# At most two of the first 24 loads in flight, in a fused decay-attention and FFN kernel

## The chip, the cores and the metric

The kernel runs on one core of one Trainium2 chip. The metric is the device time of one execution in microseconds; for the kernel before it is the median of three runs. Profiles come from one profiled execution each.

## The reference, cut to what matters

Attention with a decay per head, over blocks with a carried state, is followed by a feed-forward network with a squared relu. All is float32.

```python
# q, k, v: (4, 8, 768, 64); lam: (8,); w_in: (512, 2048); w_out: (2048, 512)
for b in range(nb):                                   # blocks of 64 positions
    intra = einsum('bhic,bhjc->bhij', qb, kb) * Dmask      # Dmask: lam ** (i - j) for i >= j
    intra = einsum('bhij,bhjd->bhid', intra, vb)
    inter = einsum('bhid,bhde->bhie', qb * lam_pow, kv_state)
    out[:, :, sl] = intra + inter
    kv_state = lam_block * kv_state + einsum('bhsd,bhse->bhde', kb * rev_pow, vb)
x = out, as (3072, 512)                               # 4 x 768 tokens, 8 heads of 64
h = maximum(x @ w_in, 0)
return h * h @ w_out
```

## The kernel before, in words

**Tiles.** The 3072 tokens are cut into 24 chunks of 128, and three chunks make one tile of 384 tokens, eight tiles in all. For a chunk, attention runs in four parts on TensorE, all on matmuls of 64x64 (L302): an opening of 64 matmuls as the profile counts them (scores and new states, `open`), and a result in two halves (`result(0, ..)` with the states' part, `result(1, ..)`). Between the opening and the result VectorE masks the scores (s, L363) and adds up the states (hold, L355, L361); ScalarE copies the first state of a sequence (hold, L354). Between the two halves of the result stands a one-element copy on ScalarE, the dot (L401). Then VectorE multiplies the result by the decay (xr, two steps, L409), and xr is split into a high and a low part (xs: ScalarE's cast L415, VectorE's subtraction L416) which are the FFN's input. Before the opening, the chunk's values are scaled by powers of lam: for the first six chunks by six steps on ScalarE (L329) and one on VectorE (L331).

**FFN.** For each tile and each of 16 slices f of the hidden size, TensorE multiplies the inputs by the slice's first weight (L433: wih high, wil low), ScalarE applies relu and square (g, gh: L447 to L452), VectorE makes the low part (gl, L454), and TensorE multiplies by the second weight (L439, L440, L442: woh, wol).

**Weights.** Each weight slice is loaded once (st, L278), 512 KB, and split into its high and low part in place: an absolute value on ScalarE (L279), four steps on VectorE (L280 to L286), a cast on ScalarE (L288) and a subtraction on VectorE (L290). There are three st and three m buffers. Tile 0 and tile 1 use the weights while they arrive.

**Loads.** All loads leave from SyncE's queue, 512 KB each: st for a weight, ka and qv for a chunk (L316, L317). The first 24 by the order of issue before: 1, 2 the two weights of slice 0; 3 to 6 ka and qv of chunks 0 and 1; 7 slice 1's first weight; 8 to 11 chunks 2 and 3; 12 slice 1's second weight; 13 to 16 chunks 4 and 5; 17, 18 slice 2's weights; 19 to 22 chunks 6 and 7; 23, 24 slice 3's weights. Besides them ScalarE loads the small table lamx, from which GpSimd makes the powers (L236, L250).

**What sets the order.** Every step is first recorded with an engine, a duration, a key (when it is due) and its buffers, and a planner (`Plan.order`) lays all of them out by list scheduling with these durations and with a latency per engine (LAT). Each engine's instructions are then written out in that order, and each engine runs its own strictly in that order, waiting on semaphores where data or buffers are needed. The planner also puts filler matmuls on zeros (L240, L243) where it sees TensorE idle before its time 140. `in_turn` keeps the loads of chunks in sequence. The semaphores of loads are eight counters in rotation (DMAHW0 to DMAHW7, the first taken by lamx), so a load also waits until the eighth load before it has landed.

Of the kernel before, what the change touches and what calls it, by code (L numbers as in the profile page):

```python
# [55 lines left out]
class Plan:  # L56


    LAT = {"PE": 0.22, "ACT": 0.14, "DVE": 0.13, "POOL": 0.12, "SP": 2.0}

    def __init__(self):
        self.ops, self.slots = [], {}
# [4 lines left out]
    def op(self, eng, dur, key, fn, deps=(), bufs=(), after=(), lat=None, mode=None):  # L67
        o = Op(eng, dur, key, fn, [d for d in deps if d is not None], list(bufs), [d for d in after if d is not None], lat or self.LAT[eng], mode)
        for b in o.bufs:
            b.left += 1  # L70
        self.ops.append(o)
        return o

    def order(self, pe_slow, fill, begin):
        need, out = {}, {}
        for o in self.ops:
            both = set(map(id, o.deps)) | set(map(id, o.after))
            need[id(o)] = len(both)
            for d in both:
                out.setdefault(d, []).append(o)  # L80
        ready = {e: [o for o in self.ops if o.eng == e and not need[id(o)]] for e in self.LAT}
        free = dict(dict.fromkeys(self.LAT, 0.0), **begin)
        slots = {k: [(0.0, i) for i in range(n)] for k, n in self.slots.items()}
# [68 lines left out]
FIRST, SLOW_STEP, LAG, BEGIN2, CHUNK, STEP = 18.0, 6.5, 16, 9.0, 3.0, 4.8  # L152
PE_SLOW, FILL_END, FILL, FILL_REST, SWITCH = 6.5, 140.0, 0.215, 0.1, 0.18
XOFF = 16
VS = 6
AFTER = NF - 2


def tt(n):

    return 0.066 + n / 960


def act(n):

    return 0.085 + n / 1200
# [6 lines left out]
def kernel(ctx: ExitStack, tc: tile.TileContext, ka, qv, lamx, w, out):  # L173
    nc = tc.nc
    const = ctx.enter_context(tc.tile_pool(name="const", bufs=1))
    ps = ctx.enter_context(tc.tile_pool(name="ps", bufs=1, space=PSUM))
    plan = Plan()
# [25 lines left out]
    mask = const.tile([P, HC], F32, name="mask")  # L203
    xs = const.tile([P, XOFF + 2 * SLOTS["x"] * NCC * N], F32R, name="xs")
    tiles["x"] = [[xs[:, XOFF + (2 * i + t) * NCC * N:XOFF + (2 * i + t + 1) * NCC * N].rearrange("p (c i) -> p c i", c=NCC) for t in range(2)] for i in range(SLOTS["x"])]
    dot = const.tile([P, 1], F32, name="dot")
# [12 lines left out]
    def at(b):  # L219
        return tiles[b.kind][b.slot]  # L220
# [14 lines left out]
    def power(hs):  # L235
        nc.gpsimd.tensor_tensor(out=wdec[:, hs], in0=lam[:, hs], in1=ej[:, hs], op=ALU.pow)  # L236
# [7 lines left out]

    plan.filler = filler

    o_start = plan.op("POOL", 4.95, -99, start_tables)
    o_pow = plan.op("POOL", 1.6, -98, lambda: power(slice(0, H)), [o_start])
    o_pow2 = plan.op("POOL", 1.6, -97, lambda: power(slice(H, 2 * H)), [o_pow])
    o_lc = plan.op("POOL", 1.01, -96, lambda: nc.gpsimd.tensor_tensor(out=lc, in0=lam[:, 2 * H:2 * H + NP], in1=ec, op=ALU.pow), [o_pow2])  # L250
# [2 lines left out]
    def turned():  # L253
# [3 lines left out]
    o = plan.op("DVE", 0.4, -5, lambda: nc.vector.tensor_copy(  # L257
        at(wb).rearrange("p (s d) -> p s d", d=D), wdec[:, H:2 * H].unsqueeze(2).broadcast_to([P, H, D])), [o_pow2], [wb])
    o_turned = o = plan.op("PE", 0.9, 3, turned, [o], [wb, rps], mode="F")
    o_rdec = plan.op("DVE", tt(512), 3, lambda: nc.vector.tensor_tensor(  # L260
        out=rdec, in0=at(rps).rearrange("p (n i) -> p n i", n=NCC), in1=lam[:, 2 * H + NP:].unsqueeze(2).broadcast_to([P, NCC, C]), op=ALU.mult), [o], [rps])

    def weights(f, i, key, load_key):
        def part(k):
            return (wih[f].rearrange("p c f -> p (c f)"), wil[f].rearrange("p c f -> p (c f)"), woh[f], wol[f])[2 * i + k]

        st, m = Buf("st"), Buf("m")

        def words(t):
            return at(st).bitcast(U32).rearrange("p (n t) -> p n t", t=2)[:, :, t]  # L270

        def bits():
            return at(m).bitcast(U32)

        def add(eng, dur, fn, deps, bufs, lat=None):
            return plan.op(eng, dur, key, fn, deps, bufs, lat=lat)

        o = plan.op("SP", 1.28, load_key, lambda: nc.sync.dma_start(out=at(st), in_=w[f, i]), [], [st])  # L278
        o = add("ACT", 0.56, lambda: nc.scalar.activation(at(m), words(1).bitcast(F32), AF.Abs), [o], [st, m])  # L279
        o = add("DVE", 0.336, lambda: nc.vector.tensor_scalar(  # L280
            out=at(m), in0=at(m), scalar1=W_MIN, scalar2=W_MAX, op0=ALU.max, op1=ALU.min), [o], [m])
        o = add("DVE", 0.336, lambda: nc.vector.tensor_scalar(  # L282
            out=bits(), in0=bits(), scalar1=3, scalar2=0x3FFFFFF8, op0=ALU.logical_shift_left, op1=ALU.bitwise_and), [o], [m])
        o = add("DVE", tt(512), lambda: nc.vector.scalar_tensor_tensor(  # L284
            out=bits(), in0=words(1), scalar=0xC0000000, in1=bits(), op0=ALU.bitwise_and, op1=ALU.bitwise_or), [o], [st, m])
        o = add("DVE", tt(512), lambda: nc.vector.scalar_tensor_tensor(  # L286
            out=bits(), in0=words(0), scalar=29, in1=bits(), op0=ALU.logical_shift_right, op1=ALU.bitwise_or), [o], [st, m])
        oh = add("ACT", act(512), lambda: nc.scalar.copy(part(0), at(m)), [o], [m])  # L288
        oh.late = f >= F_LATE
        ol = add("DVE", tt(512), lambda: nc.vector.tensor_tensor(out=part(1), in0=at(m), in1=part(0), op=ALU.subtract), [oh], [m])  # L290
        return oh, ol
# [3 lines left out]
    def in_turn(name, o):  # L295
        if turn.get(name):
            o.after.append(turn[name])
        turn[name] = o
        return o
# [4 lines left out]
    class Chunk:  # L304
# [8 lines left out]
            self.blocks = 2 if self.c < NC_ - 1 else 1  # L313

        def load(self, key):
            self.o_ka = in_turn("load", plan.op("SP", 1.28, key, lambda: nc.sync.dma_start(out=at(self.ka), in_=ka[self.i]), [], [self.ka]))  # L316
            self.o_qv = in_turn("load", plan.op("SP", 1.28, key, lambda: nc.sync.dma_start(out=at(self.qv), in_=qv[self.i]), [], [self.qv]))  # L317

        def vals(self):
            return at(self.qv)[:, 1].rearrange("p n (h d) -> p n h d", h=2)  # L320
# [4 lines left out]
        def weighted(self, key):  # L325
            v = lambda: at(self.qv)[:, 1].rearrange("p n (h d) -> p (n h) d", h=2)
            split = VS if self.i < N_ALONE else 0

# [154 lines left out]
    for f in range(NF):  # L483
        t = FIRST + f * SLOW_STEP
        ws.append((weights(f, 0, t - 7, -30 + ws_at[f]), weights(f, 1, t - 2, -30 + ws_at[f] + (3.5 if f == 1 else 0.5))))
# [3 lines left out]
    for i in range(len(CHUNKS)):  # L489
        ti, j = i // NT, i % NT  # L490
        if i < N_ALONE:
            key = i * CHUNK if ti == 0 else BEGIN2 + (i - NT) * CHUNK
        else:
            k = ti - 1 if j else max(ti - 2, 1)
            key = begin[k] + per[k] * ((0.5, 4.5, 8.5) if k == 1 and ti == 2 else (12.5, 3.5, 8.0))[j]
# [4 lines left out]
    for i, ch in enumerate(chunks):  # L500
# [4 lines left out]
        key = nxt.key if nxt else ch.key + 0.2 if i < N_ALONE else begin[ti - 1] + 12.5 * per[ti - 1]  # L505
# [55 lines left out]
```

## Time and profile before

| | before |
|---|---|
| median of 3 runs | 619.06 us (617.88 to 619.86) |
| the profiled execution | 618.99 us, its span 617.3 us |
| TensorE matmul busy | 606.9 us, 98% of the span |
| VectorE, ScalarE busy | 298.0 us (48%), 215.1 us (35%) |
| loads and stores | 49.06 MB |
| mean granted TensorE clock | 0.992 |

Busy time of TensorE is modelled and says little about where it is slow; the views by stretch of time and the chain of waits say more. In the rows quoted below a view of groups or of time gives the line in the program, the engine (PE is TensorE, PEld its weight loads, DVE VectorE, ACT ScalarE, SPq SyncE's queue), the operation, output<-input by name, and xcount.

### The profile page before, as it was taken

The page shows a single profiled execution, that of the slowest core. Times are in us where ns is not written, and L with a number is a line of the kernel's source. Part 1 is how long each engine was busy: PE and PEld are TensorE (multiplying, and loading weights), DVE is VectorE, ACT ScalarE, POOL GpSimd, SP SyncE. Part 2 cuts the span into 40 slices and gives each one's busy share as a digit, 9 for nine tenths or more (in the row PEclk, how much of TensorE's full clock was granted, in tenths as well). Part 3 has the DMA queues.
Part 4 walks back from the last instruction along what each step waited for, and adds up shares of the span by engine and source line. Part 5 has one row for each costly group of instructions (what it writes and reads, how often), then busy time and mean ns, then how long its engine had stood idle before and what let it go on. Part 6 is the DMA issues. An engine that isn't in the chain of part 4 may idle for free.

```text
span 617.3 us, 12907 instructions
## 1 busy us (share of the span) xinstructions
PE 606.9 (98%) x5686; PEld 538.4 (87%) x5686; DVE 298.0 (48%) x612; ACT 215.1 (35%) x450; POOL 5.7 (1%) x10
## 2 busy tenths in 40 slices
PE   8799999999999999999999999999999999999997
PEld 4489998888898898988899998989888989899996
DVE  6689999965233444343343442434443423232223
ACT  5547767743341222221223232222223222232221
POOL 3000000000000000000000000000000000000000
PEclk9789999999999999999999999999999999999999
DMA  8914555424020121110121120111110000010001
GB/s 342 401 48 165 175 172 179 163 103 150 30 81 29 58 69 70 51 71 20 50 70 51 70 69 1 69 52 69 71 61 36 26 1 1 2 51 1 0 2 51
DMA packets 15175, 49.06 MB, mean 79 GB/s; under 512 B 1808, under 2 KB 1808, under 8 KB 15120
## 3 DMA queue, kind: packets, MB, share of 16 engines
q1 hardware_dynamic: 14976, 48.24, 21.4%
q8 instruction: 44, 0.72, 0.5%
q14 instruction: 11, 0.09, 0.0%
q10 hardware_dynamic: 144, 0.01, 0.0%
HBM read 41.96 MB, written 6.29 MB: 78 GB/s over the span
## 4 chain that ended last, share of the span: by engine, by line
PE 96%; DMA 2%; DVE 1%; issue 1%; ACT 0%; ACTq 0%
PE bank L433 44%; PE bank L439 15%; PE bank L442 14%; PE bank L440 14%; PE bank L302 8%; DMA ka<-ka 1%; DMA g<-lamx 1%; PE bank L243 1%; DVE m L284 0%; DVE xr L472 0%; DVE s L363 0%; DVE xr L409 0%; DVE rdec L260 0%; DVE m L282 0%; DVE hold L361 0%
## 5 line engine op out<-in xcount | busy, mean ns | idle before, releaser
L433 PE MATMUL bank<-xs,wih 128*128 128x384 f32 x1024 | 200.7, 338 | 0.0
L433 PEld LDWEIGHTS bank<-xs,wih 128*128 128x128 f32 x1024 | 180.6, 188 | 6.0
L453 DVE TENSOR_TENSOR g<-g 128x384 f32<-128x384 f32 x96 | 53.5, 557 | 212.7 <-ACT gh L452 167.2
L447 ACT ACTIVATE g<-bank 128x384 f32<-128x384 f32 x128 | 62.8, 490 | 267.0 <-PE bank L433 267.0
L439 PE MATMUL bank<-woh,gh 128*128 128x512 f32 x384 | 152.3, 397 | 0.0
L440 PE MATMUL bank<-wol,gh 128*128 128x512 f32 x384 | 150.8, 393 | 0.0
L433 PE MATMUL bank<-xs,wil 128*128 128x384 f32 x512 | 110.0, 337 | 0.0
L442 PE MATMUL bank<-woh,gl 128*128 128x512 f32 x384 | 109.4, 393 | 0.0
L433 PEld LDWEIGHTS bank<-xs,wil 128*128 128x128 f32 x512 | 91.0, 188 | 0.0
L442 PEld LDWEIGHTS bank<-woh,gl 128*128 128x128 f32 x384 | 71.9, 188 | 16.4 <-DVE gl L454 0.5
L439 PEld LDWEIGHTS bank<-woh,gh 128*128 128x128 f32 x384 | 72.0, 188 | 15.0 <-ACT gh L450 0.6
L440 PEld LDWEIGHTS bank<-wol,gh 128*128 128x128 f32 x384 | 72.1, 188 | 13.6
L454 DVE TENSOR_TENSOR gl<-g,gh 128x384 fp32r<-128x384 f32 x128 | 71.2, 556 | 16.0 <-ACT gh L450 10.0
L452 ACT ACTIVATE gh<-g 128x384 fp32r<-128x384 f32 x96 | 50.3, 524 | 3.0
L355 DVE TENSOR_TENSOR hold<-bank,hold 128x256 f32<-128x256 f32 x40 | 16.8, 420 | 34.5 <-PE bank L302 34.5
L302 PE MATMUL bank<-qv,ka 64*64 64x64 f32 x1472 | 29.0, 228 | 2.4 <-issue 2.4
L415 ACT CAST xs<-xr 128x512 fp32r<-128x512 f32 x24 | 14.9, 621 | 44.2 <-DVE xr L409 44.1
L302 PEld LDWEIGHTS bank<-qv,ka 64*64 64x64 f32 x1472 | 26.8, 144 | 3.7 <-issue 3.7
L302 PEld LDWEIGHTS bank<-s,qv 64*64 64x64 f32 x768 | 17.2, 139 | 11.7 <-issue 8.7
L302 PE MATMUL bank<-s,qv 64*64 64x64 f32 x768 | 23.1, 232 | 2.7 <-issue 1.8
L331 DVE TENSOR_TENSOR qv<-qv,wdec 128x512 f32<-128x512 f32 (+1 forms) x24 | 14.1, 590 | 24.0 <-DMA qv<-qv 23.9
L279 ACT ACTIVATE m<-st 128x512 f32<-128x512 f32 x32 | 21.5, 674 | 9.4 <-DMA st<-w 8.0
(46 smaller groups left out, 300.7 us busy)
## 6 DMA issues: line engine op xcount, KB each, us to landing
st<-w SPq DMA_DIRECT2D x32, 512.0 KB, 3.4
ka<-ka SPq DMA_DIRECT2D x24, 512.0 KB, 3.9
qv<-qv SPq DMA_DIRECT2D x24, 512.0 KB, 5.2
out<-ob SPq DMA_DIRECT2D x23, 256.0 KB, 2.1
out<-xr SPq DMA_DIRECT2D x1, 256.0 KB, 2.0
g<-lamx ACTq DMA_DIRECT2D x1, 12.0 KB, 4.3
```

The source lines that it names most:

```text
L279: o = add("ACT", 0.56, lambda: nc.scalar.activation(at(m), words(1).bitcast(F32), AF.Abs), [o], [st, m])
L302: nc.tensor.matmul(*args, **kw, skip_group_check=True)
L355: return plan.op("DVE", tt(256), key, lambda: nc.vector.tensor_tensor(out=at(new), in0=u(t), in1=at(old), op=ALU.add), [o] + deps, [self.s ...
L415: oh = plan.op("ACT", act(512), key2, lambda: nc.scalar.copy(at(x)[0][:, :, cs], at(xr)), os_, [xr, x])
L433: nc.tensor.matmul(at(h)[:, 0:N], wt[:, cc, :], xt[:, cc, :], start=k == 0, stop=k == 3 * NCC - 1)
L439: nc.tensor.matmul(at(os_[j]), at(gh)[:, sl], woh[f], start=f == 0, stop=False)
L440: nc.tensor.matmul(at(os_[j]), at(gh)[:, sl], wol[f], start=False, stop=False)
L442: nc.tensor.matmul(at(os_[j]), at(gl)[:, sl], woh[f], start=False, stop=f == NF - 1)
L447: orr = plan.op("ACT", 0.49, key, lambda: nc.scalar.activation(at(g), at(h)[:, 0:N], AF.Relu), [o1], [h, g, run])
L452: ogh = plan.op("ACT", 0.525, key, lambda: nc.scalar.activation(at(gh), at(g), AF.Square), [orr], [g, gh])
L453: og = plan.op("DVE", 0.555, key, lambda: nc.vector.tensor_tensor(out=at(g), in0=at(g), in1=at(g), op=ALU.mult), [orr, ogh], [g])
L454: ogl = plan.op("DVE", 0.555, key, lambda: nc.vector.tensor_tensor(out=at(gl), in0=at(g), in1=at(gh), op=ALU.subtract), [og, ogh], [g, gh, ...
```

## The change

Three things are altered. Each load is passed through a new function `loaded`: load 3 to load 24, by the order in which they are written out, gets a wait on the landing of the load two before it. The planner's cost of a load on SyncE rises from 1.28 to 1.65 and SyncE's latency from 2.0 to 2.3; GpSimd's first step is costed at 5.2 in place of 4.95. So the planner writes another order on all engines. The work on data is the same.

```diff
-    LAT = {"PE": 0.22, "ACT": 0.14, "DVE": 0.13, "POOL": 0.12, "SP": 2.0}
+    LAT = {"PE": 0.22, "ACT": 0.14, "DVE": 0.13, "POOL": 0.12, "SP": 2.3}
...
+PACE, PACED, LOAD = 2, 24, 1.65
...
-    o_start = plan.op("POOL", 4.95, -99, start_tables)
+    o_start = plan.op("POOL", 5.2, -99, start_tables)
...
+    loads = []
+
+    def loaded(d):
+
+        loads.append(d.ins)
+        if PACE < len(loads) <= PACED:
+            tc.add_manual_dep(d.ins, loads[-1 - PACE].name, mybir.DependencyInfo(mybir.DependencyClass.Sync, mybir.DependencyReason.DATA), reason="pace")
...
-        o = plan.op("SP", 1.28, load_key, lambda: nc.sync.dma_start(out=at(st), in_=w[f, i]), [], [st])
+        o = plan.op("SP", LOAD, load_key, lambda: loaded(nc.sync.dma_start(out=at(st), in_=w[f, i])), [], [st])
...
-            self.o_ka = in_turn("load", plan.op("SP", 1.28, key, lambda: nc.sync.dma_start(out=at(self.ka), in_=ka[self.i]), [], [self.ka]))
+            self.o_ka = in_turn("load", plan.op("SP", LOAD, key, lambda: loaded(nc.sync.dma_start(out=at(self.ka), in_=ka[self.i])), [], [self.ka]))
```

The load of qv is altered as that of ka is. Lines of the program move down by one up to the new function and by nine behind it.

SyncE's queue at its start, before; the names in brackets are the landing counters and engines that a load waits for:

```order
L278 DMA st_134<-w 128x512
L316 DMA ka_0_148<-ka 128x1024
L317 DMA qv_0_154<-qv 128x1024
L316 DMA ka_1_149<-ka 128x1024
L317 DMA qv_1_155<-qv 128x1024
L278 DMA st_135<-w 128x512
L316 DMA ka_2_150<-ka 128x1024 [waits DMAHW0_49]
L317 DMA qv_2_156<-qv 128x1024 [waits DMAHW1_49]
```

And now:

```order
L287 DMA st_134<-w 128x512
L325 DMA ka_0_148<-ka 128x1024 [waits DMAHW1_49]
L326 DMA qv_0_154<-qv 128x1024 [waits DMAHW2_49]
L325 DMA ka_1_149<-ka 128x1024 [waits DMAHW3_49]
L326 DMA qv_1_155<-qv 128x1024 [waits DMAHW4_49]
L287 DMA st_135<-w 128x512 [waits DMAHW5_49]
L325 DMA ka_2_150<-ka 128x1024 [waits DMAHW6_49,DMAHW0_49]
L326 DMA qv_2_156<-qv 128x1024 [waits DMAHW7_49]
```

The order of these loads is kept; each now waits for the landing two before it, where before the eighth load before it was waited for. Further down, load 19 is now slice 3's first weight and the loads of chunks 6 and 7 are 20 to 23.

TensorE at the first FFN product (xs with wih_69 and wil_70), before; qv_4 is chunk 4's buffer, qv_3 with s_2 and s_3 the second half of chunk 3's result:

```order
L302 MATMUL bank_63<-qv_4_158,ka_4_152 64x64 x2
L302 MATMUL bank_61<-qv_4_158,ka_4_152 64x64 x2
L302 MATMUL bank_62<-s_2_122,qv_3_157 64x64 x2
L302 MATMUL bank_68<-s_3_123,qv_3_157 64x64 x2
L302 MATMUL bank_62<-s_2_122,qv_3_157 64x64 x2
L302 MATMUL bank_68<-s_3_123,qv_3_157 64x64 x2
L433 MATMUL bank_65<-xs,wih_69 128x384 x8
L433 MATMUL bank_65<-xs,wil_70 128x384 x4
```

And now:

```order
L244 MATMUL bank_63<-ob_114 64x128 x2
L442 MATMUL bank_63<-xs,wih_69 128x384 x8
L442 MATMUL bank_63<-xs,wil_70 128x384 x4
L311 MATMUL bank_62<-s_2_122,qv_3_157 64x64 x2
L311 MATMUL bank_68<-s_3_123,qv_3_157 64x64 x2
L311 MATMUL bank_62<-s_2_122,qv_3_157 64x64 x2
L311 MATMUL bank_68<-s_3_123,qv_3_157 64x64 x2
L311 MATMUL bank_61<-qv_4_158,ka_4_152 64x64 x2
L311 MATMUL bank_64<-qv_4_158,ka_4_152 64x64 x2
```

The product now stands ahead of the second half of chunk 3's result and of chunk 4's opening, which both stood before it. Ahead of it there are 30 rows of fillers in place of 23.

ScalarE at the relu of the third FFN product and the absolute value of load 24 (m_138<-st_134; g_111<-bank_68 before and g_111<-bank_66 now are relus), before:

```order
L288 CAST wih_77<-m_138 128x512
L447 ACTIVATE g_111<-bank_68 128x384
L288 CAST woh_79<-m_136 128x512
L449 ACTIVATE g_111<-g_111 128x384
L279 ACTIVATE m_138<-st_134 128x512
L450 CAST gh_107<-g_111 128x384
```

And now:

```order
L297 CAST wih_77<-m_138 128x512
L424 CAST xs<-xr_1_161 128x4x128
L288 ACTIVATE m_138<-st_134 128x512
L456 ACTIVATE g_111<-bank_66 128x384
L297 CAST woh_79<-m_136 128x512
L458 ACTIVATE g_111<-g_111 128x384
L459 CAST gh_107<-g_111 128x384
```

The absolute value that needs load 24 moved ahead of a relu, its square and the cast that follow.

More of the change, by code (lines that the diff above doesn't have):

```diff
@@ L315, in load @@
         def load(self, key):
-            self.o_ka = in_turn("load", plan.op("SP", 1.28, key, lambda: nc.sync.dma_start(out=at(self.ka), in_=ka[self.i]), [], [self.ka]))
-            self.o_qv = in_turn("load", plan.op("SP", 1.28, key, lambda: nc.sync.dma_start(out=at(self.qv), in_=qv[self.i]), [], [self.qv]))
+            self.o_ka = in_turn("load", plan.op("SP", LOAD, key, lambda: loaded(nc.sync.dma_start(out=at(self.ka), in_=ka[self.i])), [], [self.ka]))
+            self.o_qv = in_turn("load", plan.op("SP", LOAD, key, lambda: loaded(nc.sync.dma_start(out=at(self.qv), in_=qv[self.i])), [], [self.qv]))
         def vals(self):
```

## The prediction

> **What bounds the kernel now.** First the page: the span, the granted TensorE clock and the DMA share in 40 slices of 15.4 us.
>
> ```profile
> span 617.3 us, 12907 instructions
> PEclk9789999999999999999999999999999999999999
> DMA  8914555424020121110121120111110000010001
> q8 instruction: 44, 0.72, 0.5%
> ```
>
> Only the start differs from the rest: slices two and three have a lower clock, and the DMA engines are full in the first two. The last line is a DMA queue that carries instructions: 44 packets of 16.4 KB.
>
> Next the chain of waits in the first 46 us (start, length, what).
>
> ```profile
> 17.88 1.78 issue
> ...
> 20.52 3.04 PE bank L302 x103
> 23.57 2.37 issue
> ...
> 28.48 1.92 PE bank L243 x5
> ...
> 32.14 2.41 PE bank L302 x89
> 34.56 2.28 PE bank L433 x12
> ```
>
> TensorE's first FFN product (L433) starts at 34.5. Before it the chain runs through TensorE itself, and twice through "issue", in which it waited for nothing that the profile shows: 4.15 us. Busy time by stretch (PE, PEld with counts, then the other engines, clock, DMA share, GB/s) says what these two are.
>
> ```profile
> 17.88:23.58 5.70, 3.73 (x127) 3.30 (x127) 2.73 (x9) 2.81 (x10) 0.00 (x0) 0.73 1.04 412
> ...
> 20.00:25.00 5.00, 3.38 (x118) 2.96 (x111) 2.72 (x7) 3.09 (x9) 0.00 (x0) 0.66 1.03 408
> 25.00:30.00 5.00, 4.06 (x103) 2.46 (x104) 2.29 (x8) 2.64 (x10) 0.00 (x0) 0.73 1.03 406
> 30.00:35.00 5.00, 4.95 (x121) 4.01 (x118) 2.54 (x7) 2.69 (x9) 0.00 (x0) 0.58 0.23 87
> 35.00:40.00 5.00, 5.00 (x146) 4.68 (x145) 4.99 (x14) 2.40 (x6) 0.00 (x0) 1.00 0.02 3
> ```
>
> From the start of one stall to the start of the next TensorE ran 127 matmuls and 127 weight loads, 254 instructions. A packet of 16.4 KB at 0.72 MB for some 11,400 PE instructions (5,686 of each kind) holds about 258. So I read both as waits for the next block of TensorE's code, which travels on the engines that the loads keep full. The stalls end at 19.66 and 25.94, 6.3 us apart. At 35 to 40, with a DMA share of 0.02, TensorE ran more instructions (146 and 145) in 5 us without one. The second cost is the clock: 0.66, 0.73 and 0.58 granted from 20 to 35, which stretches chunks and fillers alike. After 34.5 no stall above half a microsecond is left on TensorE. The end is therefore the start of the first FFN product plus a fixed amount of work, and the change must be judged by how much is done at that time.
>
> **The loads.** SyncE's issues (start, length), and the first waits of ScalarE for a load:
>
> ```profile
> 0.79 0.85 SPq L278 DMA_DIRECT2D st<-w  x2
> ...
> 7.53 0.33 SPq L317 DMA_DIRECT2D qv<-qv  x1
> 8.89 0.33 SPq L278 DMA_DIRECT2D st<-w  x1
> 10.09 0.33 SPq L316 DMA_DIRECT2D ka<-ka  x1
> 11.36 0.33 SPq L317 DMA_DIRECT2D qv<-qv  x1
> ```
>
> ```profile
> 4.96 0.67 ACT L279 ACTIVATE m<-st 128x512 f32<-128x512 f32 x1 [2.24 <-DMA st<-w]
> ...
> 6.25 0.67 ACT L279 ACTIVATE m<-st 128x512 f32<-128x512 f32 x1 [0.63 <-DMA st<-w]
> ```
>
> Loads 1 and 2 land at 4.9 and 6.2. The four issues from 7.53 on wait for loads 3 to 6 (eight landing counters used in turn), so these land 1.28 us apart, and so on to about 31: load 9 (qv of chunk 2) near 15.2, load 11 (qv of chunk 3) near 17.8.
>
> With the change, load n leaves when load n-2 has landed. How long a load takes then is not in this trace as such; the nearest rows are the extremes over a tensor's loads, first the weights (mostly alone), then qv (each right behind a ka):
>
> ```profile
> DMA to landing us min/median/max: 3.3/3.4/11.4
> ```
>
> ```profile
> DMA to landing us min/median/max: 4.3/5.2/11.6
> ```
>
> I take 3.4, since once paced a load is issued 1.3 to 2.1 us after the other one and not right behind it, plus 0.05 for SyncE's reaction: 3.45 us a pair. The bounds are 2.56 (two at 1.28, nothing lost) and 4.3. So odd loads land at 4.9, 8.35, 11.8, 15.25, 18.7, 22.15 (load 11), even ones at 6.2, 9.65, 13.1 and so on: load 14 at 26.9, 16 at 30.35, 24 at 44.15. Load 11 is 4.35 us later than now. Behind a waiting SyncE stand only further loads; who waits for those are ScalarE and VectorE, in order.
>
> **The chain to the first FFN product**, step by step. What one step takes:
>
> ```profile
> 11.83 1.54 ACT L329 ACTIVATE qv<-qv,wdec 128x64 f32<-128x64 f32 x6
> ...
> 14.08 0.16 ACT L401 COPY dot<-bank 128x1 f32<-128x1 f32 x1
> ```
>
> ```profile
> 13.32 0.46 PE L302 MATMUL bank<-s,qv 64*64 64x64 f32 x16 [0.64 <-DVE s L363]
> ...
> 13.60 0.41 PE L302 MATMUL bank<-qv,hold 64*64 64x64 f32 x16
> ...
> 13.83 1.11 PE L302 MATMUL bank<-qv,ka 64*64 64x64 f32 x64
> ...
> 15.00 2.32 PE L243 MATMUL bank<-ob 64*64 64x512 f32 x12
> ```
>
> ```profile
> 34.71 0.74 DVE L409 TENSOR_TENSOR xr<-bank,rdec 128x256 f32<-128x256 f32 x2
> 35.37 0.41 DVE L363 TENSOR_TENSOR s<-bank,mask 128x256 f32<-128x256 f32 x1
> 35.70 0.41 DVE L355 TENSOR_TENSOR hold<-bank,hold 128x256 f32<-128x256 f32 x1
> ...
> 36.70 0.68 DVE L416 TENSOR_TENSOR xs<-xr,xs 128x512 fp32r<-128x512 f32 x1
> ```
>
> By starts: a scaling on ScalarE costs 0.26, a mask or state step on VectorE 0.33, the xr pair 0.66, an opening of 64 matmuls 1.1, a result's first half 0.5. By the new order VectorE's first step for weight 1 stands ahead of chunk 1's masks and waits for load 7: 15.25, plus ScalarE's 0.67 and 0.33, is 16.3. Mask, xr pair, hold, mask (0.33+0.66+0.33+0.41) end at 18.05. The result's second half waits for the dot, which stands behind two scalings of load 9: 18.7+0.6+0.16 = 19.45. Second half 0.4, filler 0.25, opening of chunk 2 1.1: 21.2. VectorE ends a weight step at 21.4; mask, xs, hold, mask (0.33+0.6+0.33+0.41) end at 23.1. The filler of 2.1 us there (2.32 times 0.9) ends with them. First half 0.5 and opening of chunk 3 (its six scalings end at 22.15+1.54 = 23.7) 1.1: 24.75. The dot there ends at 25.1; second half 0.4, xr pair, hold, mask 1.4: 27.0. First half and a filler 0.6, and VectorE's last xs ends at 28.1: the first FFN product starts near 28.0 against 34.5, at full clock and without code stalls.
>
> **What is not yet done then.** The new order puts the product ahead of chunk 3's second half (0.41) and chunk 4's opening (1.11), so 1.5 us of the 6.5 are only moved. All other matmuls are the same in number; the seven filler rows more stand ahead of the first product, inside the chain above.
>
> **After it.** Chunk 5's opening needs load 16: 30.35, a cast of 0.62 and six scalings end near 32.8, TensorE comes to it at 33.5. The weights:
>
> ```profile
> 53.84 0.68 DVE L290 TENSOR_TENSOR wil<-m,wih 128x512 fp32r<-128x512 f32 x1
> ```
>
> ```profile
> 56.45 0.86 PE L433 MATMUL bank<-xs,wil 128*128 128x384 f32 x4
> ```
>
> ```profile
> 49.05 0.49 ACT L447 ACTIVATE g<-bank 128x384 f32<-128x384 f32 x1 [1.44 <-PE bank L433]
> 49.47 0.62 ACT L288 CAST woh<-m 128x512 fp32r<-128x512 f32 x1
> ```
>
> Now the fourth weight's low part ends at 54.5 and is used at 56.45: 1.9 us in hand. VectorE stood idle half of 20 to 35, so it too moves ahead; in the new order 40 steps of 0.33 to 0.69 us, 17.7 together, lie from load 12's low part (31.3) to the same end, near 49; its use comes near 51. Two short waits of TensorE remain in that sum, for the first gh and gl, 0.4 us together.
>
> Sum: 6.5 - 1.5 - 0.4 = 4.6 us off the span of 617.3. The profiled execution took 618.99, 1.69 more than its span, and the median is 619.06, so both fall alike: 619.06 - 4.6 = **614.4 us**.
>
> **The rivals.**
>
> *The code still comes late, or the clock still dips: no change.* The changed kernel keeps the engines about 74% full (1.28 of 1.73 a load), and the 6.3 us between arrivals may not shrink. With both stalls kept in full the gain is 4.6 - 4.15 = 0.45: 618.6. A dip of the clock to half at the same place costs about as much: opening 1.1, filler 2.1, halves 0.9, 4.1 us in all. Against it: without loads no stall is seen, and the longest gaps that I compute on TensorE are 0.7 us, twice between 17 and 19.5. "DMA: Bandwidth & Descriptors", section Queues, rings and completion order, of the Trainium skill, says that each engine takes its queue rows in turn, packet by packet; by that the number of queued loads should not delay a code packet, and the stalls would stay. The trace speaks against it: 6.3 us between arrivals under full load. For the clock: gaps of 1.78 and 2.37 us were followed by 0.66 and 0.58. "TensorE: Matmul & The Clock Gate", Part 1, of the Trainium skill, drops the clock only after an idle window of about 3.4 us; no gap here is so long, so the trace disagrees, and the row decides. By the page nothing would dip and 614.4 stands. Chance 0.19.
>
> *The pace itself becomes the bound: slower.* With the pair at 4.3 us instead of 3.45 the first product comes five pairs, 4.25 us, later, and load 24 eleven pairs, 9.35 us, later. Load 24 matters more: its absolute value stands on ScalarE ahead of the third FFN product's relu (the order shows it). TensorE has work until about 47.3; 0.67+0.49+0.62 on ScalarE must fit before, so load 24 has until 45.5, 1.35 us in hand. The change is then 4.6 - (9.35 - 1.35) = -3.4: 622.5. It turns from gain to loss at 0.54 a pair, a pair of 4.0. For it: qv's 4.3 and the first load's 4.1 (0.79 to 4.9). Against it: 3.4 as the median of 32 loads. Chance 0.15.
>
> *The waits do nothing*, because loads land as fast as now anyway, and only the new order acts: a landing of 3.3 at the least against 2.56 for two under full load nearly excludes it. The chain keeps its steps on the engines and the code stalls come back: 618.6 as above. Chance 0.01.
>
> **How the numbers follow.** Forecast 0.65, own range 613 to 616.5: half the stalls kept (2.1 us) at one end, a pair shorter by 0.3 at the other (five pairs, 1.5 us). What a measurement here tells from no change is about 0.3%, 1.9 us; below 617.2 is faster, above 620.9 slower. The forecast's 0.65 counts as faster, of the first rival 0.01 too (half a stall kept and half a dip), the rest of it and the last one as the same; from the first rival's tail 0.01 goes to slower: faster 0.66, same 0.18, slower 0.16. At a pair of 3.1 the gain would be 6.4: 612.7, the low end. The upper end, 619.6, takes in the first rival and leaves out most of the second.
>
> **What would show it.** Right: no "issue" of over 1 us on TensorE before 30, granted clock near 1 from 20 to 35, loads 1.7 us apart, the first L433 at 27 to 29.5, TensorE full after it. Wrong: L433 later than 33, or ScalarE waiting for st near 44 with TensorE idle behind it.

## The result and the profile after

| | before | after |
|---|---|---|
| median, same chip, 6 executions each | 619.14 us (617.86 to 619.86) | 624.31 us (623.66 to 627.89) |
| ratio after to before, 95% interval | | 1.0099 (1.0072 to 1.0126) |
| the profiled execution, its span | 618.99, 617.3 us | 623.8, 622.1 us |
| first FFN product starts | 34.49 us | 34.55 us |

The changed kernel is slower by 1%; the prediction said 614.4 us. The lines of the page after:

```profile
span 622.1 us, 12919 instructions
...
PEclk9699999999999999999999999999999999999999
DMA  7775455514120221020121110212210100010001
```

The DMA engines stood at 0.8 and 0.9 in two slices and at 0.1 in the third; now they stand at 0.7 in all three. Busy time by stretch (engines, then clock, DMA share, GB/s):

```profile
15.00:20.00 5.00, 3.67 (x88) 2.38 (x88) 2.52 (x7) 2.67 (x10) 0.00 (x0) 1.00 0.69 236
20.00:25.00 5.00, 4.07 (x102) 2.93 (x106) 4.04 (x10) 2.64 (x9) 0.00 (x0) 0.60 0.76 245
25.00:30.00 5.00, 5.00 (x68) 2.52 (x64) 3.25 (x8) 2.97 (x9) 0.00 (x0) 0.50 0.73 250
```

The share fell from 1.03 to about 0.75, as forecast, but the clock from 20 to 30 is no better than before (0.60 and 0.50, where 0.66 and 0.73 stood). SyncE's issues; the load of each row leaves when the load two before it has landed:

```profile
4.87 0.33 SPq L325 DMA_DIRECT2D ka<-ka  x1
6.13 0.33 SPq L326 DMA_DIRECT2D qv<-qv  x1
...
17.58 0.33 SPq L326 DMA_DIRECT2D qv<-qv  x1
19.39 0.33 SPq L325 DMA_DIRECT2D ka<-ka  x1
21.85 0.33 SPq L326 DMA_DIRECT2D qv<-qv  x1
...
26.19 0.33 SPq L325 DMA_DIRECT2D ka<-ka  x1
...
34.87 4.68 SPq L287 DMA_DIRECT2D st<-w  x3
```

These are loads 3, 4, 9, 10, 11, 13 and 17 to 19. Load 7 landed at 17.58 (its row frees load 9), load 9 at 21.85, load 11 at 26.19. From load 3 to load 17 are 30.0 us for seven pairs: **4.29 us a pair**, 2.14 us a load, where 3.45 and 1.73 were forecast.

What that does on the engines, first at load 7, a weight. ScalarE, VectorE and TensorE in turn:

```profile
17.65 0.67 ACT L288 ACTIVATE m<-st 128x512 f32<-128x512 f32 x1 [1.09 <-DMA st<-w]
```

```profile
18.35 0.43 DVE L289 TENSOR_SCALAR m<-m 128x512 f32<-128x512 f32 x1 [2.48 <-ACT m L288]
```

```profile
20.49 0.46 PE L311 MATMUL bank<-s,qv 64*64 64x64 f32 x16 [1.74 <-DVE s L372]
...
25.59 3.84 PE L244 MATMUL bank<-ob 64*64 64x512 f32 x10
...
34.55 0.61 PE L442 MATMUL bank<-xs,wih 128*128 128x384 f32 x2
```

The absolute value waits for the load, VectorE's weight step waits for it with the masks of a chunk queued behind it, and TensorE stands 1.74 us for such a mask. Then the clock is halved, and ten fillers take 3.84 us. The first FFN product starts where it did before.

The second place is load 24. From 23.8 on the chain of waits runs through loads alone up to it:

```profile
45.41 4.48 DMA ka<-ka
...
49.96 4.25 DMA st<-w
...
54.29 0.67 ACT m L288
54.96 0.38 ACT g L456
```

ScalarE and TensorE there:

```profile
54.29 0.67 ACT L288 ACTIVATE m<-st 128x512 f32<-128x512 f32 x1 [6.08 <-DMA st<-w]
54.86 0.47 ACT L456 ACTIVATE g<-bank 128x384 f32<-128x384 f32 x1
```

```profile
56.86 0.50 PE L448 MATMUL bank<-woh,gh 128*128 128x512 f32 x1 [2.05 <-ACT gh L459]
```

ScalarE stands 6.08 us for load 24 with the relu behind it, and TensorE 2.05 us for what the relu makes. The 4.8 us of span more are then: first product +0.06; work only moved behind it 1.5, as forecast; this wait 2.05; and 1.2 that is left over. The moved work, the second half of chunk 3's result and chunk 4's opening, stands right behind the first product's last matmuls (36.04):

```profile
36.83 0.46 PE L311 MATMUL bank<-s,qv 64*64 64x64 f32 x16
37.11 1.11 PE L311 MATMUL bank<-qv,ka 64*64 64x64 f32 x64
```

The page shows a part of the 1.2 as weight loads of the second product that wait for gh and gl (0.6 and 0.5 us in these two groups before, 2.8 and 2.0 now, some of it the wait just told):

```profile
L448 PEld LDWEIGHTS bank<-woh,gh 128*128 128x128 f32 x384 | 72.2, 188 | 17.1 <-ACT gh L459 2.8
L451 PEld LDWEIGHTS bank<-woh,gl 128*128 128x128 f32 x384 | 71.6, 188 | 17.7 <-DVE gl L463 2.0
```

One part of the forecast did come: no "issue" of over 0.25 us is left before TensorE's matmuls up to 35. The stalls of 1.78 and 2.37 us for code are gone.

### The profile page after: what moved, and what is told of

Its sections match the earlier page's. It is cut to its first block, busy times and chain, and to the rows that moved or that the text cites. A ratio compares the mean times of both kernels' runs of the same rounds, so it can differ in the third digit from the quotient of the medians.

```text
span 622.1 us, 12919 instructions
## 1 busy us (share of the span) xinstructions
PE 611.9 (98%) x5700; PEld 540.0 (87%) x5700; DVE 299.5 (48%) x612; ACT 215.5 (35%) x450; POOL 5.9 (1%) x10
## 4 chain that ended last, share of the span: by engine, by line
PE 88%; DMA 8%; DVE 2%; ACT 1%; issue 0%; SPq 0%; ACTq 0%
PE bank L442 41%; PE bank L448 14%; PE bank L451 14%; PE bank L449 14%; PE bank L311 6%; DMA st<-w 3%; DMA ka<-ka 3%; DMA qv<-qv 2%; DVE m L293 0%; DVE m L295 0%; DVE gl L463 0%; DVE wol L299 0%; DVE m L291 0%; DVE wil L299 0%; DVE m L289 0%
## 5 line engine op out<-in xcount | busy, mean ns | idle before, releaser
L448 PEld LDWEIGHTS bank<-woh,gh 128*128 128x128 f32 x384 | 72.2, 188 | 17.1 <-ACT gh L459 2.8
```

The source lines that it names most:

```text
L448: nc.tensor.matmul(at(os_[j]), at(gh)[:, sl], woh[f], start=f == 0, stop=False)
```

## The experiments

Two theories stood after the result. **P**: the pace costs the time, since two loads under way move only 240 GB/s and every chunk and weight comes later. **O**: the new order costs it, since it puts steps that need a load ahead of others, and the pace itself is harmless. Edits are against the changed kernel. All times are medians; each ratio is against the kernel before, run on the same chip (618.44 us for the first four kernels, 618.60 for the next four, 618.85 for the last four).

| kernel | us (range) | ratio (95%) | span | first product | clock |
|---|---|---|---|---|---|
| pace only, old order | 626.05 (625.18 to 627.29) | 1.0122 (1.0102 to 1.0143) | 624.1 | 40.59 | 0.989 |
| new order only | 615.09 (614.66 to 615.76) | 0.9943 (0.9928 to 0.9958) | 613.0 | 28.79 | 1.000 |
| four under way, old order | 617.88 (615.8 to 619.55) | 0.9986 (0.9972 to 1.0000) | 614.1 | 31.75 | 0.990 |
| two, first 16 loads only | 624.92 (622.63 to 626.18) | 1.0097 (1.0072 to 1.0122) | 623.6 | 34.83 | 0.988 |
| two, planned with 2.2 us | 620.00 (619.06 to 620.95) | 1.0024 (1.0013 to 1.0035) | 618.1 | 31.61 | 1.000 |
| three, new order | 613.45 (611.9 to 618.67) | 0.9930 (0.9908 to 0.9953) | 611.1 | 26.71 | 1.000 |
| four, new order | 615.51 (614.79 to 616.56) | 0.9952 (0.9933 to 0.9971) | 614.0 | 28.80 | 1.000 |
| new order, no pace, no later fillers | 617.40 (616.19 to 618.47) | 0.9984 (0.9974 to 0.9995) | 615.9 | 29.21 | 0.990 |
| one, new order | 659.04 (658.85 to 659.23) | 1.0646 (1.0608 to 1.0684) | 657.1 | 49.71 | 0.960 |
| three, old order | 617.38 (616.16 to 618.6) | 0.9974 (0.9958 to 0.9990) | 614.7 | 30.41 | 0.994 |
| three, SyncE's latency 3.3 | 616.88 (614.65 to 618.29) | 0.9964 (0.9948 to 0.9980) | 615.4 | 28.94 | 0.999 |
| two, one weight load ahead | 622.27 (621.77 to 623.42) | 1.0058 (1.0038 to 1.0077) | 620.0 | 32.01 | 0.997 |

Span, first product and clock are those of the one profiled execution.

**The two halves of the change, each alone.** First the pace with the planner's old numbers:

```diff
-    LAT = {..., "SP": 2.3}
+    LAT = {..., "SP": 2.0}
-PACE, PACED, LOAD = 2, 24, 1.65
+PACE, PACED, LOAD = 2, 24, 1.28
-    o_start = plan.op("POOL", 5.2, ...)
+    o_start = plan.op("POOL", 4.95, ...)
```

> The waits of the change with the planner's numbers of before, so the old order on every engine. Theory P (the pace: two loads in flight land only one per 2.2 us, as the changed kernel's profile shows): load 11 lands near 26, load 16 near 37, load 24 near 54 as in the changed kernel, no code stall above 1 us on TensorE, the first FFN product near 36 to 38 (chunk 4's opening stands ahead of it here), and a time of 621 to 627. Theory O (the new order is what costs): the pace without the new order removes the code stalls and costs little, 614 to 618.

Measured 626.05: 7.6 us slower than before. TensorE's waits in it:

```profile
17.14 0.70 PE L311 MATMUL bank<-s,qv 64*64 64x64 f32 x16 [2.33 <-DVE s L372]
...
26.85 0.46 PE L311 MATMUL bank<-s,qv 64*64 64x64 f32 x16 [3.52 <-ACT dot L410]
...
34.05 0.66 PE L311 MATMUL bank<-s,qv 64*64 64x64 f32 x16 [2.42 <-ACT dot L410]
```

Each stands before a result that needs what SyncE now brings later, and the first product comes at 40.59, 6.1 us late (36 to 38 was expected; the clock also falls to 0.50 three times before it, from 17.1, 27.3 and 34.2). Then the order alone, with no wait at all:

```diff
-PACE, PACED, LOAD = 2, 24, 1.65
+PACE, PACED, LOAD = 2, 0, 1.65
```

> The planner's new numbers and so the new order, but none of the paced waits. Theory P: loads land 1.28 us apart again, load 24 near 33, the two code stalls of together about 4 us return and the first FFN product comes at 31 to 34; no wait of ScalarE for load 24; 617 to 620. Theory O: the order alone costs, 622 to 626.

Measured 615.09, 3.4 us faster than before. Its chain and its stretch with full DMA engines:

```profile
22.67 1.41 issue
...
28.86 2.28 PE bank L442 x12
```

```profile
20.00:25.00 5.00, 3.60 (x112) 2.14 (x103) 3.84 (x10) 3.56 (x11) 0.00 (x0) 1.00 1.02 405
```

One code stall is left and the clock stays at 1.00. The order is the half that gains; theory O falls. Theory P holds for the pace, but its 617 to 620 for this kernel is missed too: one stall, not two, came back, and the clock did not dip. The pace adds 7.6 us to the old order, and 8.5 to the new one (from 3.4 less to 5.2 more, each against the kernel before on its own chip).

**How many loads under way.** Four, with the old order (the three edits of the first kernel, and PACE 4):

> Four loads in flight in place of two, in the old order. Theory P, with landing time set by how much is in flight: twice the loads in flight give 410 GB/s or close to it, a load per 1.3 to 1.5 us, and the code has half as long a queue: code stalls of 0 to 2 us in all; 614 to 618. If the code's wait does not depend on how many loads are in flight: stalls as before, 619 to 620. Theory O: any pace is harmless in the old order, 614 to 618.

Measured 617.88, the same as before within 0.3%. Two stalls, smaller than before together, and the issues of loads 5 and 14, 11.52 us for nine loads:

```profile
17.68 1.78 issue
...
23.72 0.90 issue
```

```profile
4.77 0.33 SPq L325 DMA_DIRECT2D ka<-ka  x1
...
16.29 0.33 SPq L326 DMA_DIRECT2D qv<-qv  x1
```

At 1.28 us a load, four under way fill the engines as eight did; the waits change little there.

Three and four with the new order (`PACE, PACED, LOAD = 3, 24, 1.65` and `4, 24, 1.65`):

> Three loads in flight, new order. If a landing takes about 4.4 us when others are under way, three in flight give a load per 1.5 us (345 GB/s): load 11 near 20, load 24 near 40, code stalls below 1.5 us in all, first FFN product near 29 to 30, 615 to 618. If the rate does not rise over that of two in flight: 622 to 625.

> Four in flight, new order. Loads 1.28 us apart as with four in the old order. If a shorter queue of loads shortens the code stall that is left in the new order (1.41 us without pace): below 1 us, first FFN product near 28 to 28.5, 614 to 615. If it does nothing: 615.1 as the order alone.

Four measured 615.51, about what no pace gives, with two stalls:

```profile
26.64 1.55 issue
...
38.52 1.09 issue
```

Three measured 613.45, faster than the kernel before and the changed one, and below the 615 to 618 that was expected. Its issues of loads 8 and 23, and a stretch:

```profile
10.16 0.33 SPq L325 DMA_DIRECT2D ka<-ka  x1
...
35.01 0.35 SPq L326 DMA_DIRECT2D qv<-qv  x1
```

```profile
20.00:25.00 5.00, 4.89 (x132) 2.66 (x128) 4.79 (x14) 3.79 (x13) 0.00 (x0) 1.00 0.92 306
```

24.85 us for 15 loads is 1.66 us a load, at a share of 0.92, and from 10 to 50 TensorE has no stall of over 0.25 us in the chain and no dip of its clock. Its ten executions scatter more than others: eight lie from 611.9 to 615.6 with a mean clock of 0.999 or 1.000, two at 616.61 and 618.67 with 0.997 and 0.992. The interval overlaps that of the order alone (0.9928 to 0.9958), so that three are better than no pace isn't shown. Three with the old order (the first kernel's edits, PACE 3):

> Three in flight, old order. If the gain of three in flight comes from the code (stalls below 1 us in all) and the clock: 614.5 to 617. If it needs the new order's fillers and places: clock 0.5 to 0.8 in part of 20 to 35, 617 to 620.

Measured 617.38, 1.5 us faster than before; no stall over 0.51 us is left, but its clock is at 0.50 from 20 to 25. And one under way, as the other end of the scale (`PACE, PACED, LOAD = 1, 24, 1.65`):

> One load in flight, new order: what a load takes with nothing beside it. If a load alone lands in 3.4 us, as the least landing in every profile has it, and two in flight slow each other down to 4.4: issues 3.45 us apart, load 11 lands near 38, 640 us or more. If a paced load takes 4.4 us whatever is beside it: issues 4.4 us apart and load 11 near 48, 650 or more.

Measured 659.04. Loads 3 to 5, each alone:

```profile
7.90 0.33 SPq L325 DMA_DIRECT2D ka<-ka  x1
11.38 0.33 SPq L326 DMA_DIRECT2D qv<-qv  x1
14.89 0.33 SPq L325 DMA_DIRECT2D ka<-ka  x1
```

This is the landing of 3.4 us, with 0.05 for the reaction, on which the prediction rested: it holds for a load that has the engines to itself.

**The pace on the first 16 loads only** (`PACE, PACED, LOAD = 2, 16, 1.65`):

> The change as it is, but only loads 3 to 16 are paced; 17 to 24 leave freely. Theory P with the second half of the loss in load 24: load 24 lands near 47 or earlier in place of 54.2, ScalarE's wait of 6 us for it shrinks below 1 us, TensorE's 2.05 us wait near 55 goes, and the first FFN product stays near 34.5: 620 to 622 in place of 624.3. If load 24 is not what costs after 50 us: 623.5 to 625.

Measured 624.92, no gain over the change. Seven of the last eight loads leave by 38.85, and the stalls come back just then. Load 24 itself leaves only at 49.25: it waits for a buffer that VectorE frees, and VectorE stands behind the second stall. So it lands at 52.8, not at 47; even so ScalarE's wait for it is down from 6.08 us to 1.16, and TensorE's 2.05 us are gone. Two stalls of 2.83 us together have taken their place. ScalarE, the chain, and a stretch:

```profile
52.85 0.69 ACT L288 ACTIVATE m<-st 128x512 f32<-128x512 f32 x1 [1.16 <-DMA st<-w]
```


```profile
40.80 0.73 issue
...
45.35 2.10 issue
```

```profile
40.00:45.00 5.00, 4.27 (x127) 3.47 (x129) 4.84 (x12) 4.05 (x9) 0.00 (x0) 1.00 1.00 370
```

The order is that of the change and so is the pace of the first 16 loads; TensorE stalls for code in the stretch in which the share is 1.00 and right behind it, and has no "issue" of over 0.25 us before its matmuls up to 35.

**The true pace planned** (SyncE's latency 2.2, a load costed at 2.2):

```diff
-    LAT = {..., "SP": 2.3}
+    LAT = {..., "SP": 2.2}
-PACE, PACED, LOAD = 2, 24, 1.65
+PACE, PACED, LOAD = 2, 24, 2.2
```

> The change with the planner told what two loads in flight cost on the chip: 2.2 us a load and 2.2 us behind it in place of 1.65 and 2.3; load 24's absolute value then stands later on ScalarE. If the loss is partly a plan made for a pace that the chip does not hold: no wait of ScalarE above 2 us for a weight and no 2 us wait of TensorE near 55, clock dips smaller, 620 to 622.5 (624.3 for the change). If the pace alone costs, whatever the plan: 623.5 to 627.

Measured 620.00: 1.4 us behind the kernel before, where the change is 5.2 behind. The clock stays whole. ScalarE waits for a weight 0.24 us at 42.0 and 0.74 us at 56.2, and 1.75 us for a chunk's qv at 32.5; TensorE's matmuls wait no longer than 0.4 us at a time between 16 and 60:

```profile
25.00:30.00 5.00, 4.92 (x195) 3.41 (x191) 3.08 (x8) 3.33 (x12) 0.00 (x0) 1.00 0.80 228
```

```profile
31.61 1.66 PE L442 MATMUL bank<-xs,wih 128*128 128x384 f32 x8
```

Its product comes 2.9 us earlier than before's, but some 1.7 us of fillers and 2 us of chunk work stand behind it that stood ahead. So 3.8 us of the change's loss go away when the order is planned for 2.2 us a load in place of 1.65, which keeps the clock whole as well; how much of the 3.8 is the clock isn't told apart.

**The fillers** (new order, no pace; no fillers planned after 12 us: `FILL_END` 140.0 to 12.0 and `PACED` 24 to 0; the 20 filler rows left out work on zeros, so the output is the same):

> The new order without paced waits and without the fillers after the planner's time 12 (20 rows of matmuls on zeros left out, which leaves the output as it is). If the granted clock between 15 and 35 us hangs on the fillers: it falls to 0.5 to 0.7 in part of it, and the first FFN product comes 1 to 3 us later: 616 to 618. If the clock follows the waits alone, or does not matter for the chain: 614 to 615.5.

Measured 617.40: of the 3.4 us that the order gains 1.2 are left without these fillers, in all ten executions with a clock of 0.989 to 0.993 where that had 1.000. The first product and its stretch:

```profile
29.21 2.93 PE L442 MATMUL bank<-xs,wih 128*128 128x384 f32 x8
```

```profile
25.00:30.00 5.00, 3.48 (x94) 3.17 (x87) 3.72 (x10) 2.32 (x9) 0.00 (x0) 0.50 0.15 57
```

Eight matmuls take 2.93 us that take 1.66 at full clock. The gain of the order alone thus rests largely on TensorE being kept busy enough for its clock.

**Three, with the latency that three show** (`PACE` 3 and SyncE's latency 3.3):

> Three in flight, and the planner's latency behind a load raised from 2.3 to 3.3, so that it counts on the 4.95 us that a load takes with three in flight. If the plan's fit to the true landing is worth something here as it was with two in flight: 611 to 613. If not: as three in flight in the new order, 613.5.

Measured 616.88, a miss: 2.0 us faster than before, where three with the numbers of the change are 5.2 faster. Code stalls are back, 0.74 at 27.59 and 0.83 at 38.57, 1.6 of the 4.3 us between the two spans; why they come back at the same number of loads wasn't found.

**Load 24's place.** Chunk 6's first load is put behind slice 3's second weight, which so becomes load 20:

```diff
-    loads = []
+    loads, load_ops = [], {}
...
+        load_ops[f, i] = o
...
+            if self.i == N_ALONE:
+                self.o_ka.after.append(load_ops[3, 1])
```

> The change as it is (two in flight, all 24 paced), but slice 3's second weight is loaded ahead of chunks 6 and 7: it becomes load 20. If ScalarE's wait for that weight is what costs TensorE after 50 us: it lands near 50 or earlier in place of 54.2, TensorE's wait of 2 us near 55 goes, the first FFN product stays at 34.5: 621 to 622.5. If the late weight does not set TensorE's time: 623.5 to 625.

Measured 622.27: 3.4 us behind the kernel before, 1.8 better than the change. ScalarE at that weight and TensorE:

```profile
49.36 0.68 ACT L289 ACTIVATE m<-st 128x512 f32<-128x512 f32 x1 [1.31 <-DVE m L292]
```

```profile
25.43 2.32 PE L244 MATMUL bank<-ob 64*64 64x512 f32 x10
...
32.01 1.66 PE L446 MATMUL bank<-xs,wih 128*128 128x384 f32 x8
...
40.46 0.46 PE L312 MATMUL bank<-s,qv 64*64 64x64 f32 x16 [1.38 <-DVE s L376]
```

ScalarE's 6.08 us for the weight are down to 1.31 (load 20 lands at about 49.3, just ahead of it), and TensorE's 2.05 us near 55 are gone, but a new gap of 1.38 us stands at 40.46, where a chunk now comes later. And up to 25.4 TensorE does the same as in the changed kernel, with fillers that take 2.32 us in place of 3.84: in this profiled execution the dip of the clock was shorter (22.67 to 26.09 in place of 20.97 to 31.21), and the product comes 2.5 us earlier. At a mean clock of 0.989 to 0.992 four executions of this kernel took 622.0 to 623.4 us and four of the changed one 623.7 to 626.0, so some of the 1.8 us is not the clock; how much can't be told from these runs. A good part of the wait was passed on to the chunks.

## Why the prediction was wrong, point by point

**The loads' pace: the step that failed.** "I take 3.4, since once paced a load is issued 1.3 to 2.1 us after the other one and not right behind it, plus 0.05 for SyncE's reaction: 3.45 us a pair." Measured: 4.29 us a pair (loads 3 to 17), a landing of 4.34 for load 11 (21.85 to 26.19). The upper bound, 4.3 from qv's fastest landing, was the true value. The argument that a gap of 1.3 to 2.1 us between two issues makes them land as one alone was not in any row: the weights' median of 3.4 came mostly from loads that had the engines to themselves. In the changed kernel the loads leave 1.3 to 2.6 us apart; load 3 alone still lands in 3.5 us (4.87 to 8.36), loads 4 to 16 take 4.2 to 4.8. Load 7 came 2.3 us later than forecast, load 11 4.0, load 24 10.1 (54.2 against 44.15). Both signs of being wrong that the prediction named were there: the product later than 33, and ScalarE waiting for a weight with TensorE idle behind it, though at 48 to 54 and not near 44.

**The chain to the first product.** From load 11's landing to the product the forecast has 5.85 us (22.15 to 28.0). The kernel with one weight load ahead, whose clock dips for 3.4 us only, takes 6.0 (25.99 to 32.01), so with load 11 4.0 us late the forecast's 28.0 becomes 32.0. The changed kernel takes 8.4 (26.19 to 34.55). There TensorE at half its clock sets the time, and no longer load 11: chunk 3's scalings end at 27.74, its opening starts at 30.14. So the steps and their durations were about right for a clock that stays up, and the other 2.5 us are the clock. Where loads keep up the product comes near the forecast or ahead of it: 28.79 with no pace and 28.80 with four, each with a stall of 1.4 to 1.6 us in it, 26.71 with three.

**"A fixed amount of work" behind the first product.** Span less first product is 582.8 before and 582.4 with four under way in the old order; with the 1.5 us moved taken off it is 582.7 for the order alone and 582.9 for three. It did not hold everywhere: 584.3 with three in the old order, which has a stall of 0.51 behind the product, and 585.2 without the later fillers, where the product itself runs at half clock. In the changed kernel it is 3.2 us more than before.

**The moved 1.5 us** are in the rows (0.46 and 1.11). **The 0.4 us of new waits** became 3.2: 2.05 for load 24 and 1.2 that the rows show only in part.

**The second rival was the case.** It named the place (the absolute value for load 24, ahead of the third product's relu on ScalarE), the pair (4.3) and the price: 622.5. Measured 624.31. It had a chance of 0.15. Its loss is load 24's lateness less 1.35 us in hand; with the 10.1 us measured that is 8.7, and the rows have 8.6: the product 6.55 us later than forecast and TensorE's 2.05 us behind it. So the mechanism was right. It had not seen the clock dip; by the same sum that cost little on top, since TensorE would else have waited longer for load 24, but no run shows this alone. The row that spoke for it was that of qv, and loads 9 and 11, on which the chain hangs, are qv; the row taken was that of the weights.

**The first rival was half the case**: the code stalls did go, against it, and the clock did dip. Computed gaps of 0.7 us on TensorE had spoken against the dip, but those came from the pace of 3.45: load 7's 2.3 us made one of 1.74 us.

**The code stalls.** That they are waits for code the traces show directly. In the fourteen profiles TensorE has 13 stalls of over 0.5 us for which no other releaser is seen, and each ends 1.25 to 1.55 us after a 16 KB packet of the instruction queue q8 has ended (before: packets end at 18.26 and 24.50, stalls at 19.66 and 25.94). That loads bring them on is seen in the old order: the stalls add up to 4.15 us before, 2.68 with four under way, 0.51 with three, none with two. With two in the new order they return at 40 to 47, where the last eight loads are let go. The number under way is not all, though: in the new order there are 1.41 us with no pace, 2.64 with four, and with three none or 1.57, depending on the plan. Each sum is from one execution, and that of four in the old order is the fastest of its ten. "DMA: Bandwidth & Descriptors" of the Trainium skill, section Queues, rings and completion order, has each engine switch between queue rows packet by packet; by that two or eight waiting loads should leave a code packet alike. The old order's rows disagree. The packets themselves are not stretched: the two ahead of the stalls before took 1.07 and 1.11 us, two with few loads beside them 1.27 (37.81) and 0.88 (41.73). What makes them come late isn't shown.

**The clock.** A gap of 1.74 us (18.75 to 20.49) was followed by 0.60 and 0.50 for ten us. "TensorE: Matmul & The Clock Gate", Part 1, of the Trainium skill, gives the drop after an idle window of about 3.4 us, counted by a window that runs freely. No gap here is that long, so on the idle window the trace disagrees again; on its length it agrees, since the granted clock changes in these traces only at steps of 3.41 us (20.52, 23.93, 27.35 and 34.17 before; 20.97 and 31.21 now). In the window ahead of the drop TensorE's matmuls fill 49% here, and 39% and 41% before. The stalls of 1.41 us (order alone) and 1.55 us (four, new order) left 59% and 62% of theirs, and no drop followed. A limit is not shown by this: three in the old order dropped after 57%. The prediction had seen in the rows of before that a shorter gap is enough and was right to let them decide; it missed the gap.

**What stays open**: what delays the code packets, at what share of a window the clock drops, why the executions of three under way scatter, why the planned latency of 3.3 brings stalls back, and the share of the clock in the last experiment.

## What to carry to other kernels

A limit on loads under way is a limit on bandwidth: measure the landing at that number under way before planning with it, and don't take it from loads that ran alone. Where loads delay something else (here TensorE's code), try the smallest limit that still moves nearly all bytes: three gave the lowest time here, though that it beats no limit isn't shown. Try the order that such a change brings without the limit too: here it gained 3.4 us by itself, where three under way gained 1.5 us in the old order and two lost in both. After such a change follow the last paced load to its reader and to what is queued behind it on that engine: that is where the delay adds up.

## What the hardware showed that was not expected

The rate by the number of 512 KB loads under way, each from the issues of one kernel:

| under way | us a load | from | GB/s |
|---|---|---|---|
| 1 | 3.49 | 7.90 to 14.89, 2 loads | 150 |
| 2 | 2.14 | 4.87 to 34.87, 14 loads | 245 |
| 3 | 1.66 | 10.16 to 35.01, 15 loads | 316 |
| 4 | 1.28 | 4.77 to 16.29, 9 loads | 410 |

Eight under way, before, move no more than four. The second load adds only 63% to the rate of the first, and a landing rises from 3.4 us (one) over 4.3 (two) to 5.0 (three, 3 x 1.66) and 5.1 (four). "DMA: Bandwidth & Descriptors" of the Trainium skill, section Latency and other measured facts, gives the fixed part of a DMA as smaller when memory is lightly loaded; the direction agrees with these rows, the size is theirs alone.
